# A gated linear recurrence and an MLP on one core: products of token pairs by seven half products, one buffer for the gates, the first pair in two halves

## The chip, the cores and the metric

The kernel runs on one core of a Trainium2 chip. A core has engines that run side by side, each with its own queue in order: TensorE (PE; its weight loads are listed apart as PEld), VectorE (DVE), ScalarE (ACT), GpSimd (POOL), and SyncE (SP), whose queue issues the DMA transfers here. Matrix products go from the on-chip memory SBUF into the accumulators of PSUM, which VectorE and ScalarE read. The metric is the device time of one launch in microseconds, the median of the runs. Before the change it is 813.15 us (three runs, 810.71 to 813.49).

## The reference

Two blocks follow each other. The first is a recurrence for each of 4 batches and 8 heads, over 768 tokens with vectors of 48; its state is a complex 48 x 48 matrix:

```
mag = np.sqrt(a_re * a_re + a_im * a_im)
scale = np.minimum(mag, 0.999) / (mag + 1e-06)
a_re_n, a_im_n = (a_re * scale, a_im * scale)
for t in range(S):
    new_re = ar * S_re - ai * S_im
    new_im = ar * S_im + ai * S_re
    S_re, S_im = (new_re + k[t] (outer) v[t], new_im)
    y[:, :, t] = np.einsum('bhd,bhde->bhe', q[:, :, t], S_re)
```

Its output, as 3072 tokens of 384 numbers, is the input x of the second, an MLP with 2048 features and an own slope for negative values of each feature:

```
h = x @ w_in                                        # 3072 x 384 by 384 x 2048
g = np.maximum(h, 0.0) + alpha * np.minimum(h, 0.0)
return (g @ w_out).astype(np.float32)               # by 2048 x 384
```

All of it is in 32-bit floating point; the large weights arrive as 64-bit words and are turned to 32 bits in the kernel.

## The kernel before

The tokens are cut into 24 units of 128 (six for each batch). Work is written as tasks, Python generators that emit one step at each call:

- `gates` (line 229), nine tasks: for one, two or three units at a time they load the decays `a_re` and `a_im` into the tile `gate`, compute phases and magnitudes with some twenty steps on VectorE and as many on ScalarE, and store phases (`phs`, line 313) and decays with their running products (`decs`, line 350) in DRAM. Most tasks cover three units, half of a batch. The tile has two buffers, so that task g waits only for task g - 2.
- `loads` and `loads_v`: for each unit q and k (tile KQ), the phases (PP), the decays (T) and the rows of v (V and VL).
- `pieces` and `weights`: sixteen pieces of w_in and w_out are loaded into three staging regions (line 410) and turned to 32 bits by ScalarE and VectorE. The regions lie in `g_sb`, the tile that holds the features later.
- `unit` (line 560), one for each unit: VectorE rotates q and k (lines 576, 578) and multiplies decays on at six levels (line 634), TensorE meets keys and queries at each level (line 593, tile ps_lv), masks are put on, keys are transposed (line 705) and multiplied with v (line 717, ps_kv); VectorE brings the state forward (lines 746, 749). The output y of a unit gathers in the PSUM tile ps_y. In the kernel before, four products of zeros open that tile (line 728), then come the 96 products of the masks with v (line 737), and last the products of the states with q (line 761), in two halves: the second needs the state after 64 tokens, so VectorE's line 749. ScalarE copies y out, and it goes to DRAM.
- `loads_x` brings y back as x, with features in the partitions.
- `all_mlp` runs over groups of one or two units (one, one, ten pairs, one, one). `features` (line 809) makes 16 blocks of 128 features for a group: three products into ps_h, then ScalarE (line 816) and VectorE (line 818) make g in `g_sb`. `outputs` (line 828) multiplies a block of one unit with 128 rows of w_out, all 384 columns wide, and sums 16 of them in ps_o; ScalarE copies the sum out (line 838).

The order of all steps is fixed by the string `ORDER`: each letter calls the next step of one task (A to I the gates, J to L the loads, M to O the weights, P to Z and a to m the units, n the x loads, o the MLP). An engine runs its own steps in that order, and waits for what it needs with semaphores. The `R` table names buffers of the planner that made the string; on the chip, the number of buffers of a tile sets what can be reused when.

Of the kernel before, what the change touches and what calls it, by code (L numbers as in the profile page):

```python
# [9 lines left out]
F32 = mybir.dt.float32  # L10
# [3 lines left out]
BF16 = mybir.dt.bfloat16  # L14
# [5 lines left out]
P = 128  # L20
# [11 lines left out]
    "ABAMBMAAAABBAAAAABAAAAAAABMAAAMNNAANBBBBBAAAKKJJJMAAAMJANAAJAAAAAAAABBOBAAONNOOBBBBBOBBBBNNOMOONBPPP"  # L32
    "LJOCKJLLCPCCCNONONPCPPPBBLLLKMMMLLKKBBJBOCPCPNNPBCCPBCBBBBBPPPPNCNBNPNNCPJJLLLLLJLLMJPCBNNPPPNBNBBBP"
    "OPPPPOCOOCPCPPOPPPPPPPMCCNOOOCOOPPDJJJMJJJDCCNNNQDPDODNPPPPDPPQNQCOPQQQQNQCPPMJJMQCOQOQNODOQQDQOJCLL"
    "LMLLLLLQDQNOOCNOORORRRnCLLLLLLLMQDRQRQRQQQQQCRRQQQQDJJKJJJMKoQoQQQoQQQLLLLLLLDONCNRNCCRNOQQOOCQCCQCC"
    "RQRCROCRQNoooooQoDQRQQDoCLooLQooQCLLLLLLRODDDRRRRRoDOoRooooooNRRRRoooRRoNDDDRoooRoRRoRoRRNRSoRSNoDRO"
    "oMJJSoooNooooooRRNSoNNoRRJJRRSSSNooooooooooSSSooooSoSSooODSSoooooSSoOoNooooJJSSnooSoSOSSLJLLLLoooRRL"
    "LLoSDSSTToJLJLLLLLLJEJToSSoSooSOSoTSToOoooTDDDDoOTooooooSSSSSSTTSSSoSToooJJKLLJLLLLoooooTSSSSSTooTTD"
    "ooooToELJJLLooooDoToooooooTDDooooooooTDTTooJLLLJoToooToooUooooooLLUoooDTTTTTooooooooooooooooooooToDD"
    "ooTooDEToooooELTJJJnTooEoTTTDTTToTDDTTTDDooooVUTTEoooooTTTLLFJoEUooUUUVUVLLLooJJoJLLLLJoooUooUoooooo"  # L40
    "ooUooooooUUUooooUUUoooooVoVoUUoooUUoVUUUEooUVEUVoUooUooUoooUoVVEEoEVKJLLLLLUUUUUUUFLLLLLJKKUUUUEVUUU"
    "UVooooooEEooooVVooVoVEEooooVoEoKVoooooooooLLLLLLLLLLVVoEVVoVEoWVoonJJEVVVVooVEEVWVooooooVVVVVVVWoEEo"
    "JLLLLEJLLLEEooooEoWVVVWVWoWEWVEVooVVLLVVoooooWWooooJooEWFooooooooooWWFFLEWEJJJKJLLLJJLLooooooWWWXooo"
    "ooWWWWoXoooooWWWWWFWooWEEFEXEEEoFoooooWWoXooWWWWWWXXoJELLLJLooXWXXXLGLJLoooWWoooXWLLLooXWWXooLXXWWXW"
    "WXoooooooLXXXXXXXXXoooooLLoooooXoXWLGJJoXXooXXXXXoYXoGXYYXooooonJLLJJLKKKLJYoXooYYYYFXXFFYoXXoooYFoo"
    "ooooooYXXFoFoKXJoYYoooGYoYoYFYXFoooooooooFGLLLJLLLLJJJJLLLoooooYYYYYooZoooooZYFFYoooooJLoooYYoFoooYY"
    "ooZGooFFFoooYooZYZZZZoooooooJFFFZYYYYYZFLLLLZLLLFYYYYYYYYYYYoooooooooaYFFFaLLLJoJLJoLLJLLKoooooooKKJ"
    "JJFZZZoooooooZZFZooooooGooZZZZZZZooZZoZooZFFFoaGGooZZooGoaZZZZZoZFZFoFFZFnLLLLLooooooooaZZZZZZZZaGGa"
    "aaZbLFLooooooaooooooaobboooHHJLooaaooooaoooooooabaaooooLJJJLLLLLJoJoooooaaaaaaaaoooaoaooaGGHGaaHoooo"
    "ooooooGbGboGGoooooooaaaaaaaabaaaaaoGboobLLJbboooGbLaaJJHHoooooLLLLLJLLJJLoLoooobcoooooobbGoobbbcbooo"  # L50
    "ooccooooobooHooooobccbbbbbbccooHbbcbooooooooocboobLLLboocGGJnJccbobbbLGGGocbbbdcccdbooooobboLLLLLLLL"
    "LLGGGGGbbbbbobLLLLooccGcoooooocJJJcoHooooococccoGococooooccooooooHoccccccGGGGGcccccccoLLJJJJKLddoGoo"
    "HoGLLLoddoddHdccoccdoooooooooooodeooddodoHdHHdoooooodeoooJJLLLLLLLJJLLJJoooooooodddHHdeoooddoHdoHHed"
    "ddoooeeeedoooIIooddooododdddHddHnddHdddoddooHeeooooddJoooooooIeeeeeoHHeooooooofoeLLdLooooeoeeeoeeeee"
    "ooooJJHJLLLLLoLLLLLLLJJJeoeoofooffoeooJoffofofffooeooooofHHHooeoeIeeeeeeHeeeeeeIgIeIoooooooffooooffo"
    "oooogHffHooHoooooofffoffffHoooeLeLLLLJJLLLLLLLLLLJJJnfJgffooooooooooofoooHgffoggffooofgIJoIHHHHHHogg"
    "gooooofffgffffggffofofgoIggfgoooooIoooooooogghhIIoooooooIogfLLLfhhoooooooIoKLLLJJhJJJJJLLLLLLLLooooh"
    "ooooIIoggoooogohhhhoghggoogoooogoioooggoogggggohggggIIIIooooooggIoggoIooooigLLLgLLLLJJLJhhhJLKoooooo"
    "ooLhhhJJoIJohooooooooooooooohhoooLLLLLihoooohihhhhoohooooiiohhooIIInIohooooooohhhhhhLiihhhhhhhhhhhoo"
    "ooooooiooIIIiioohJJLLLLLLLJJLLLLLLJoooooooIooiiooooooooooiooooiiooooooIiooooooiiIIiiiioiiIooooooojjj"  # L60
    "iooooooIooiooooooijoooijjJJjkooiLikIiooooiiiijjjjoooooiIIiiooooijLLLLLIijiiLoojjjioiLiLijLooooLoLLoo"
    "oojjjoojjjoooojjjooojjooooooojooJLjLLJoojjjjjjjjjJJJJjjjjookjjjjkooooooLookkkkkkooookooooooookkkoook"
    "noooLLLLLJJJLLJLLJJLLLLooooooLllooookkooooooooookkkkkkoooolooookkoookookooookkkoooooookkkkkkkkolllll"
    "lloooooooooooooooooollkkkLlklllJLLLLLLLLLLLoLJoooooooLooookkkkknooooolllooololoooooooooooolllllllJLJ"
    "oooooolooooollloooooooooooooooooollllooooooooolooooooooooooooooooooooooooommmoooooomommmLLLLoooooooo"
    "mmmoooLooooooooooooooooooomolllllllloooommooLlLLlmoooooooooooomnLLLLLmmoooooooooooooooooommmoooooooo"
    "oooommmmmmmooooooooomoooooooooooooooLoooooooooooooooooooooomoooooomooooomoommmmoommmmmmmoooooommmnoo"
    "oooooooooooooooooooooooooooooooooooooooooooooooooooooooooooooooooooooooooooooooooooooooooooooooooooo"
    "ooooooooooooooooooooooooooooooo")
# [28 lines left out]
def kernel(  # L98
# [99 lines left out]
    def step(*args, **kwargs):  # L198
# [5 lines left out]
        KQ=3, PP=1, T=2, V=1, WQ=2, W=1, St=3, xT=2, raw0=1, raw1=1, raw2=1, g0=0, g1=0, g2=0, ot=2, top=2,  # L204
        lv=2, misc=1, y=1, h=2, o=1).items()}
# [3 lines left out]

    scr_of = {}  # L210
# [17 lines left out]

    def gates(g, b, c0, c1):
# [7 lines left out]
        flat = work.tile([P, 6 * NK * GT + 2 * NK], F32, tag="gate", name="gate", bufs=2)  # L237
# [9 lines left out]
        for z, src in ((rows3(x), a_re), (y, a_im)):  # L247
            rows = src[b].rearrange("n i d s -> (n i d) s").rearrange("(t p) s -> p t s", p=P)
            t = yield DMA(N / 2, ("gates", g - 2))
            if last:  # L250
                nc.gpsimd.memset(z[:, :, n - 1:n], 0.0)
            nc.sync.dma_start(z[:, :, 0:n - last], rows[:, :, c0 * P + 1:c1 * P + 1 - last])
            if z is y:
                ty = t
            else:
                tx = t
# [112 lines left out]
    g_sb = consts.tile([P, 3, 6 * MT], F32, tag="g_sb")  # L369

    def region(i):
        return (i + 2) % 3

    def raw_done(name, f, e):

        i = 2 * f + (name == "out")
        for _ in range(6 if i >= NF - 3 else 1):
            R[("g" if i >= NF - 3 else "raw") + str(region(i))].put(e)
# [4 lines left out]
    def pieces():  # L383
# [17 lines left out]
        for f in range(NF // 2):  # L401
            for name, src in (("in", wi), ("out", wo)):
                t = yield DMA(788 if words else 394, takes=(R[f"raw{region(2 * f + (name == 'out'))}"],))
                raw = g_sb[:, region(2 * f + (name == "out"))]
# [148 lines left out]
    nothing = consts.tile([P, D // 2], F32, tag="nothing")  # L553
    nc.gpsimd.memset(nothing, 0.0)
    nothing = nothing.bitcast(BF16)

    sizes = [1, 1] + [MC] * ((NU - 4) // MC) + [1, 1]
    group_of = [(g, c) for g, n in enumerate(sizes) for c in range(n)]

    def unit(u):  # L560
# [159 lines left out]
        for s in range(2):  # L720
            for part in range(2):
                ev = yield PE(0.335 if s or part else 0.44, ("V", u), *(made if not (s or part) else ()), takes=() if s or part else (R["y"],), mode=2, n=12 if s or part else 14)
                if not (s or part):
                    Y = ps.tile([P, 2, 512], F32, tag="y", name="ps_y")[:, :, 0:2 * P].rearrange(
                        "p i (s t) -> p i s t", s=2)
                    for e_ in range(2):
                        for i in range(2):
                            nc.tensor.matmul(Y[64 * e_:64 * e_ + D, i].rearrange("p s t -> p (s t)"),
                                             lhsT=nothing[64 * i:64 * i + 64], rhs=ident.bitcast(BF16)[64 * i:64 * i + 64],
                                             start=True, stop=False)  # L730
                Vp = L["Vp"]
                for h in LEVELS[3 * part:3 * part + 3]:
                    for e_ in range(2):
                        for i in range(2):
                            o = halves(Y[64 * e_:64 * e_ + D, i, s], h)[:, :, 1]
                            a = A[h][64 * i:64 * i + 64, 2 * s + e_]
                            nc.tensor.matmul(o, lhsT=Vp[h][64 * i:64 * i + 64, s, e_ * D:(e_ + 1) * D],  # L737
                                             rhs=a, start=False, stop=False)
        for name in ("V", 1, 4, 16, 32):
            R[name].put(ev)  # L740
# [11 lines left out]
        if not last:  # L752
            state[b] = states[2]
        done["state", u] = k_

        g, cg = group_of[u]
        for s in range(2):
            before, known = states[s]
            e = yield PE(0.47, q_, known, mode=1, n=8)
# [161 lines left out]
```

## Time and profile before

| what | value |
|---|---|
| median of three runs | 813.15 us (810.71 to 813.49) |
| the profiled execution | 812.23 us |
| its span | 810.5 us |
| TensorE busy | 697.3 us, 86% |
| VectorE busy | 564.4 us, 70% |
| ScalarE busy | 457.0 us, 56% |
| mean DMA rate | 161 GB/s |
| granted TensorE clock, mean | 0.975 |

Busy times are unions of an engine's instructions within the span. The ends of matmuls are modelled, so the distance between the starts of neighbours says more about their pace than their durations. A 32-bit product is listed as two records. The time of the execution is 1.7 us more than the span.

### The profile page before, as it was taken

The page shows a single profiled execution, that of the slowest core. Times are in us where ns is not written, and L with a number is a line of the kernel's source. Part 1 is how long each engine was busy: PE and PEld are TensorE (multiplying, and loading weights), DVE is VectorE, ACT ScalarE, POOL GpSimd, SP SyncE. Part 2 cuts the span into 40 slices and gives each one's busy share as a digit, 9 for nine tenths or more (in the row PEclk, how much of TensorE's full clock was granted, in tenths as well). Part 3 has the DMA queues.
Part 4 walks back from the last instruction along what each step waited for, and adds up shares of the span by engine and source line. Part 5 has one row for each costly group of instructions (what it writes and reads, how often), then busy time and mean ns, then how long its engine had stood idle before and what let it go on. Part 6 is the DMA issues. An engine that isn't in the chain of part 4 may idle for free.

```text
span 810.5 us, 26318 instructions
## 1 busy us (share of the span) xinstructions
PE 697.3 (86%) x11488; PEld 522.7 (64%) x11488; DVE 564.4 (70%) x799; ACT 457.0 (56%) x897; POOL 11.9 (1%) x49
## 2 busy tenths in 40 slices
PE   0014167899999999999999999999999999999998
PEld 0013155678777667767777777777777777777776
DVE  6889998878898778786787977887466455154122
ACT  8999894775667447746574558454644333222221
POOL 4000000000000000000000000000000000000000
PEclk9998578999999999999999999999999999999999
DMA  8989998687778596677548765784653743301010
GB/s 231 292 271 249 247 235 225 152 231 200 183 203 212 161 241 141 171 196 176 148 116 228 189 164 139 200 175 114 175 121 101 166 99 100 75 12 36 28 31 10
DMA packets 177578, 130.58 MB, mean 161 GB/s; under 512 B 66296, under 2 KB 168824, under 8 KB 177016
## 3 DMA queue, kind: packets, MB, share of 16 engines
q1 hardware_dynamic: 177464, 128.91, 60.9%
q8 instruction: 90, 1.47, 0.8%
q14 instruction: 24, 0.20, 0.1%
HBM read 100.52 MB, written 35.42 MB: 168 GB/s over the span
## 4 chain that ended last, share of the span: by engine, by line
PE 67%; ACT 14%; DVE 8%; DMA 6%; issue 3%; SPq 2%; POOL 0%; ACTq 0%; DVEq 0%; POOLq 0%
PE ps_o L828 26%; PE ps_h L809 26%; PE ps_lv L593 5%; PE ps_y L737 3%; DVE KQ L634 3%; PE ps_y L761 2%; PE ps_kv L717 2%; DMA T<-decs 2%; PE ps_kt L705 2%; ACT WQ L657 1%; DMA VL<-vsc 1%; DMA PP<-phs 1%; DMA g_sb<-in_w_in_dram 1%; ACT top L426 1%; DVE gate L304 1%
## 5 line engine op out<-in xcount | busy, mean ns | idle before, releaser
L809 PE MATMUL ps_h<-xT,w_in_sb 128*128 128x256 f32 (+1 forms) x1344 | 301.2, 355 | 0.0
L828 PE MATMUL ps_o<-w_out_sb,g_sb 128*128 128x384 f32 x768 | 296.2, 497 | 4.2 <-DVE g_sb L818 3.5
L809 PEld LDWEIGHTS ps_h<-xT,w_in_sb 128*128 128x128 f32 x1344 | 233.1, 192 | 71.3 <-DVE g_sb L818 1.8
L818 DVE SCALAR_TENSOR_TENSOR g_sb<-g_sb,al,ps_h 128x256 f32<-128x256 f32 (+1 forms) x224 | 97.6, 438 | 160.5 <-ACT g_sb L816 160.0
L816 ACT ACTIVATE g_sb<-ps_h 128x256 f32<-128x256 f32 (+1 forms) x224 | 78.4, 352 | 190.9 <-PE ps_h L809 189.9
L634 DVE TENSOR_TENSOR KQ<-KQ,T 96x1024 f32<-96x1024 f32 x120 | 145.9, 1217 | 48.4 <-PE ps_lv L593 38.0
L828 PEld LDWEIGHTS ps_o<-w_out_sb,g_sb 128*128 128x128 f32 x768 | 135.5, 190 | 53.9 <-DVE g_sb L818 6.2
L593 PE MATMUL ps_lv<-WQ 96*32 96x32 f32 x2304 | 34.4, 202 | 56.0 <-DVE WQ L576 38.8
L593 PEld LDWEIGHTS ps_lv<-WQ 96*32 96x32 f32 x2304 | 26.3, 115 | 78.1 <-DVE WQ L576 32.9
L657 ACT COPY WQ<-KQ 96x1024 f32<-96x1024 f32 x48 | 49.9, 1040 | 25.5 <-DVE KQ L634 25.5
L775 ACT COPY T<-ps_y 48x256 f32<-48x256 f32 x96 | 31.6, 364 | 39.7 <-PE ps_y L761 38.9
L737 PE MATMUL ps_y<-A,VL 64*48 64x64 f32 x2304 | 43.8, 225 | 7.3 <-issue 3.7
L607 ACT ACTIVATE A<-ps_lv,columns 128x64 f32<-128x64 f32 x144 | 37.5, 337 | 20.1 <-PE ps_lv L593 20.0
L737 PEld LDWEIGHTS ps_y<-A,VL 64*48 64x48 f32 x2304 | 40.2, 126 | 10.8 <-issue 6.5
L673 ACT COPY W<-KQ 96x512 f32<-96x512 f32 x48 | 30.6, 638 | 28.3 <-DVE KQ L634 27.2
L593 PE MATMUL ps_lv<-KQ,W 96*32 96x32 f32 x1536 | 24.2, 203 | 25.3 <-ACT W L673 24.9
L593 PEld LDWEIGHTS ps_lv<-KQ,W 96*32 96x32 f32 x1536 | 19.4, 114 | 27.8 <-ACT W L673 26.2
L705 PE MATMUL ps_kt<-ident,KQ 96*128 96x96 f32 x192 | 26.0, 260 | 13.0 <-ACT T L708 6.7
L705 PEld LDWEIGHTS ps_kt<-ident,KQ 96*128 96x128 f32 x192 | 20.9, 147 | 23.8 <-ACT T L708 9.1
L707 ACT COPY T<-ps_kt 128x384 f32<-128x384 f32 x48 | 23.1, 480 | 18.8 <-PE ps_kt L705 18.6
L717 PEld LDWEIGHTS ps_kv<-V,T 64*64 64x64 f32 x1408 | 26.6, 142 | 9.5 <-ACT T L708 5.0
L617 DVE TENSOR_TENSOR A<-ps_lv,mask 128x512 f32<-128x512 f32 x48 | 32.7, 681 | 0.0
(85 smaller groups left out, 696.5 us busy)
## 6 DMA issues: line engine op xcount, KB each, us to landing
T<-decs SPq DMA_DIRECT2D x48, 384.0 KB
PP<-phs SPq DMA_DIRECT2D x24, 387.0 KB
KQ<-in_q_dram SPq DMA_DIRECT2D x48, 192.0 KB
phs<-gate SPq DMA_DIRECT2D x14, 577.5 KB
decs<-gate SPq DMA_DIRECT2D x7, 1152.0 KB
KQ<-in_k_dram SPq DMA_DIRECT2D x40, 192.0 KB
vsc<-in_v_dram SPq DMA_DIRECT2D x24, 288.0 KB
VL<-vsc SPq DMA_DIRECT2D x48, 144.0 KB
```

The costliest lines, as they stand in the source:

```text
L593: nc.tensor.matmul(t[64 * i + j:64 * i + j + HC // 2, p], lhsT=keys(n, g), rhs=queries(n, g), start=True, stop=True)
L607: nc.scalar.activation(a[:, :, cols], t[:, :, at:at + name], AF.Copy, scale=s)
L617: nc.vector.tensor_tensor(out=a.rearrange("p l n (g t) -> p l n g t", g=2), in0=t.unsqueeze(3).to_broadcast(whole), in1=pairs[first].rearr ...
L634: nc.vector.tensor_tensor(out=x, in0=x if x0 is None else x0, in1=m, op=ALU.mult)
L657: nc.scalar.copy(z.rearrange("p i n t -> p i (n t)").rearrange("p i (m h) -> p m i h", h=h), bass.AP(tensor=KQ.tensor, offset=KQ.offset + ...
L705: nc.tensor.transpose(t[:, p], KQ[:, 1, 4 * i + p], ident[:D2, :D2])
L717: nc.tensor.matmul(kv[s][j:j + HC, n], lhsT=T[rows, n, j:j + HC], rhs=V[rows, n // 2, (n % 2) * D:(n % 2 + 1) * D], start=True, stop=True)
L737: nc.tensor.matmul(o, lhsT=Vp[h][64 * i:64 * i + 64, s, e_ * D:(e_ + 1) * D], rhs=a, start=False, stop=False)
L809: nc.tensor.matmul(p, lhsT=w_in_sb[:, f // 2, kk, f % 2 * P:(f % 2 + 1) * P], rhs=x_of[m][:, kk], start=(kk == 0), stop=(kk == NK - 1))
L816: nc.scalar.activation(gt, p, AF.Relu, scale=-1.0)
L818: nc.vector.scalar_tensor_tensor(out=gt, in0=gt, scalar=al_1[:, f:f + 1], in1=p, op0=ALU.mult, op1=ALU.add)
L828: nc.tensor.matmul(sums[0], lhsT=gt[:, c * P:(c + 1) * P], rhs=w_out_sb[:, f], start=(f == 0), stop=(f == NF - 1))
```

## The change

Five things are changed together, and the order string is new.

1. For the pairs of units from the third on, the output product is made by a scheme of seven products for a 2 x 2 block product. The two units of the pair are the two block rows of the left matrix, the lower and upper eight feature blocks its columns; w_out is cut into lower and upper features and left and right 192 output columns. Four sums of g blocks (1024 columns each, VectorE) and four differences of weight blocks (made once) feed seven products of 8 x 192 columns; VectorE adds the results up in seven folds, ScalarE copies the first. Both halves of ps_o take turns.
2. The groups are now twelve pairs. The first pair goes through the first eight feature blocks a unit at a time, with its output sums for these kept in `partial`; then the other eight follow for both units, and VectorE adds the two parts.
3. Staging of the weights has four regions, in a shared tile that also holds g, the sums and the differences, and no longer lies over g.
4. The gates have one buffer; the first two tasks share it. Task g waits for task g - 1.
5. The products of zeros are gone: the state products open ps_y, and the 96 products with v follow them.

The core of the diff:

```
-"ABAMBMAAAABBAAAAAABAAAAAAABMAAAMNNAANBBBBBAAAKKJJJMAAAMJANAAJAAAAAAAABBOBAAONNOOBBBBBOBBBBNNOMOONBPPP"
+"ABMABAABAABAAAAABAAAMMMMJAAAAABBAABJNAABJJMBNNAABAKAAKLLLLAAMLMANNAAANAAAAAAANNNNANNBBBBBBBLBBBOOOBB"
...
-        flat = work.tile([P, 6 * NK * GT + 2 * NK], F32, tag="gate", name="gate", bufs=2)
+        if g == 1:
+            flat = room[0][:, 6 * N // C + 2 * NK:]
+        else:
+            flat = room[0] = work.tile([P, GATE], F32, tag="gate", name="gate", bufs=1)
...
-            t = yield DMA(N / 2, ("gates", g - 2))
+            t = yield DMA(N / 2, *[("gates", i) for i in ((0, 1) if g == 2 else (g - 1,)) if g > 1])
...
-    g_sb = consts.tile([P, 3, 6 * MT], F32, tag="g_sb")
-    def region(i):
-        return (i + 2) % 3
+    shared = consts.tile([P, 7 * F2 * P + 3 * F2 * HALF], F32, tag="shared")
+    def region(name, f):
+        i = (2 * f + (name == "out")) % 4
+        at = 18 * MT + i * 4 * DM
+        return R[f"raw{i}"], shared[:, at:at + 4 * DM]
...
-                    for e_ in range(2):
-                        for i in range(2):
-                            nc.tensor.matmul(Y[64 * e_:64 * e_ + D, i].rearrange("p s t -> p (s t)"),
-                                             lhsT=nothing[64 * i:64 * i + 64], rhs=ident.bitcast(BF16)[64 * i:64 * i + 64],
-                                             start=True, stop=False)
...
             for n in range(H):
                 nc.tensor.matmul(Y[64 * (n % 2):64 * (n % 2) + D, n // 4, n // 2 % 2, HC * s:HC * (s + 1)],
                                  lhsT=before[:, n], rhs=KQ[:, 0, n, HC * s:HC * (s + 1)],
-                                 start=False, stop=(s == 1 and n // 2 % 2 == 1))
+                                 start=not s and n // 2 % 2 == 0, stop=False)
...
+    blocks = [(0, f, c, 1) for c in range(MC) for f in range(EARLY)] + [(0, f, 0, MC) for f in range(EARLY, NF)] + [
+        (m, f, 0, MC) for m in range(1, FIRST) for f in range(NF)]
...
+    def twist():
+        for name, dst, x, y, op in (("T3", T3, B22, B12, ALU.subtract), ("T2", T2, T3, B11, ALU.add),
+                                    ("T4", T4, B21, T2, ALU.subtract)):
+            for i in range(2):
+                some = slice(i * F2 // 2, (i + 1) * F2 // 2)
+                nc.vector.tensor_tensor(out=dst[:, some], in0=x[:, some], in1=y[:, some], op=op)
...
+        def product(a, w, name, after):
+            if not bank:
+                bank.append(ps.tile([P, 2, HALF], F32, tag="o", name="ps_o"))
+                bank.append(0)
+            z = bank[0][:, bank[1] % 2]
+            bank[1] += 1
+            for i in range(F2):
+                e = yield PE(0.345, after, known.get(name), takes=() if i else (R["sums"],))
+                nc.tensor.matmul(z, lhsT=a[:, i], rhs=w[:, i], start=i == 0, stop=i == F2 - 1)
+                if i == F2 // 2 - 1:
+                    yield 0
+            return z, e
+        def fold(to, z, e, base, *deps, last=True):
+            t = yield DVE(HALF, e, *deps)
+            STT(out=to, in0=z, scalar=four, in1=base, op0=ALU.mult, op1=ALU.add)
...
+        z, e1 = yield from product(A11, B11, "P1", half)
+        TT(out=apart, in0=A11, in1=A21, op=ALU.subtract)
+        nc.scalar.activation(p1, z, AF.Copy, scale=four)
+        TT(out=A21, in0=A21, in1=A22, op=ALU.add)
+        TT(out=A11, in0=A21, in1=A11, op=ALU.subtract)
+        z, e = yield from product(A12, B21, "P2", full)
+        STT(out=ot[:, 0, 0:HALF], in0=z, scalar=four, in1=p1, op0=ALU.mult, op1=ALU.add)
+        TT(out=A12, in0=A12, in1=A11, op=ALU.subtract)
+        z, e = yield from product(A11, T2, "T2", s2)
+        t2 = yield from fold(u2, z, e, p1, t1)
+        z, e = yield from product(A21, B12, "T1", s2)
+        t3 = yield from fold(v, z, e, u2, t2)
+        z, e = yield from product(apart, T3, "T3", s3)
+        STT(out=ot[:, 1, 0:HALF], in0=z, scalar=four, in1=u2, op0=ALU.mult, op1=ALU.add)
+        tz = yield from fold(ot[:, 1, HALF:DM], z, e, v, t3, ty)
+        z, e = yield from product(A22, T4, "T4", s4)
+        ty = yield from fold(ot[:, 1, 0:HALF], z, e, ot[:, 1, 0:HALF], ty)
+        z, e = yield from product(A12, B22, "P3", s4)
+        t = yield from fold(ot[:, 0, HALF:DM], z, e, v, t3)
```

In the new order a half product (four of the eight) stands between feature blocks of later groups; after the last feature block the remaining six products of the last pair follow each other.

## The prediction

> **What bounds the kernel now.** I read the page first: engine shares, then the span in slices.
>
> ```profile
> span 810.5 us, 26318 instructions
> ...
> PE 697.3 (86%) x11488; PEld 522.7 (64%) x11488; DVE 564.4 (70%) x799; ACT 457.0 (56%) x897; POOL 11.9 (1%) x49
> ...
> PE   0014167899999999999999999999999999999998
> ...
> DVE  6889998878898778786787977887466455154122
> ACT  8999894775667447746574558454644333222221
> ```
>
> TensorE is nearly idle in the first seven slices (some 140 us), while ScalarE and VectorE are at 8 and 9; from then on it is at 9 to the end. So two stages: a start that VectorE, ScalarE and the loads set, and a long stage that TensorE sets. The stretches of 20 us confirm it (PE, PEld, DVE, ACT, POOL, then granted clock, DMA share and GB/s):
>
> ```profile
> 80.00:100.00 20.00, 3.06 (x160) 2.55 (x160) 18.40 (x20) 18.25 (x23) 0.11 (x1) 0.50 0.95 255
> ...
> 220.00:240.00 20.00, 19.58 (x377) 15.04 (x372) 18.48 (x22) 13.40 (x30) 0.11 (x1) 1.00 0.73 182
> ...
> 700.00:720.00 20.00, 20.00 (x145) 14.59 (x144) 6.79 (x12) 3.23 (x9) 0.00 (x0) 1.00 0.11 27
> ```
>
> The clock is 1.00 in the long stage, VectorE is 18.48 of 20 us busy in one stretch without hurting TensorE, and late in the run VectorE has two thirds of its time free. The chain in order of time gives the pace of the large products, with no gap between neighbours:
>
> ```profile
> 470.04 1.29 PE ps_h L809 x6
> 471.34 1.29 PE ps_o L828 x4
> ```
>
> Six records of 256 columns or four of 384 are 1536 columns in 1.29 us: 0.84 ns a column and record, two records a product. The costs of what is added come from the groups by shape (busy us, mean ns, then idle):
>
> ```profile
> L809 PE MATMUL ps_h<-xT,w_in_sb 128*128 128x128 f32 x384 | 58.5, 284 | 0.0
> ...
> L634 DVE TENSOR_TENSOR KQ<-KQ,T 96x1024 f32<-96x1024 f32 x120 | 145.9, 1217 | 48.4 <-PE ps_lv L593 38.0 <-ACT WQ L657 9.2 <-ACT T L775 1.1
> L818 DVE SCALAR_TENSOR_TENSOR g_sb<-g_sb,al,ps_h 128x256 f32<-128x256 f32 x160 | 75.7, 476 | 105.4 <-ACT g_sb L816 105.1
> ...
> L818 DVE SCALAR_TENSOR_TENSOR g_sb<-g_sb,al,ps_h 128x128 f32<-128x128 f32 x64 | 21.9, 344 | 55.2 <-ACT g_sb L816 54.9
> ```
>
> The timeline of the last unit and of the end gives what a handover costs:
>
> ```profile
> 770.12 0.30 PE L728 MATMUL ps_y<-ident,nothing 64*48 64x256 bf16 x4
> 770.25 1.55 PE L737 MATMUL ps_y<-A,VL 64*48 64x64 f32 x96
> 771.46 0.55 DVE L749 TENSOR_TENSOR St<-St,ps_kv 96x384 f32<-96x384 f32 x1
> ...
> 805.06 0.30 PEld L828 LDWEIGHTS ps_o<-w_out_sb,g_sb 128*128 128x128 f32 x2
> 805.17 1.83 PE L828 MATMUL ps_o<-w_out_sb,g_sb 128*128 128x384 f32 x4
> 805.37 0.28 ACT L816 ACTIVATE g_sb<-ps_h 128x128 f32<-128x128 f32 x1 [1.04 <-PE ps_h L809]
> 805.68 0.35 DVE L818 SCALAR_TENSOR_TENSOR g_sb<-g_sb,al,ps_h 128x128 f32<-128x128 f32 x1 [0.97 <-ACT g_sb L816]
> 806.09 0.30 PEld L828 LDWEIGHTS ps_o<-w_out_sb,g_sb 128*128 128x128 f32 x2 [0.72 <-DVE g_sb L818]
> ```
>
> The stream of a finished product ends at 805.17, its reader starts 0.20 us later; TensorE loads 0.06 us after VectorE ends, and multiplies 0.11 us after that.
>
> **The change, part by part** (span 810.5 us, run 812.23 us, so 1.7 us lie around the span; the median of the runs shown is 813.15, 0.9 us above the profiled run).
>
> *Seven products for pairs.* Features are as many columns as before. The output product was 768 records of 384 columns; it becomes 128 of 384 (two pairs kept as they were) and 1120 of 192: 294,912 columns become 264,192. 30,720 x 0.84 ns = **-25.8 us**, on TensorE's path. If instead each narrow record went at the mean of a weight load, about 0.19 us, where 192 columns need 0.161, 1120 x 0.03 = 33 us would be added, +8 in all. I take -25.8: in the tail six records of 128 columns take about 0.66 us, 0.11 each, so loads do not set the pace even there.
>
> VectorE gains, per pair, four sums of 1024 (1.22 us, the row of L634) and seven folds of 192 out of PSUM (0.41, between 0.344 and 0.476): 7.75 us, 77 in ten pairs. Eight operations of 768 on the weights at 0.95 (the gate row of that width) are 7.6; the first pair's two additions 1.2; fewer narrow evictions -4.5. Together +82 on 564, while ScalarE loses 24 copies of 0.49 and gains 14. Beside TensorE this is free as long as VectorE keeps up. In the written order, VectorE's work between the starts of units 8 and 18, summed from row means, rises from 222 to 269 us (sums of means exceed busy time by 7%, so 251 busy), against 269 us of TensorE work between the ends of the same units. At the best stretch's 92% that needs 272 us; at 89%, the mean over 20 to 160 us, 282. **+4**, ends 0 and +13; nearer the first because a good stretch is already shown in the long stage.
>
> The two halves of a product's output tile share one PSUM bank, and in the compiled order each product's first matmul waits for the fold of the product just before it, not of the one before that. A handover costs 0.20 + 0.41 + 0.06 + 0.11 = 0.78 us. Of 69 boundaries, 64 have at least a feature block (1.29 us) between; five, all in the last pair, have nothing: 5 x 0.78 = 3.9. 23 have just one block, and there a sum of 1.22 us ahead in VectorE's queue uncovers at most 0.71: 0 to 16 us. **+6**, ends +4 and +20, near the low end since most folds do not meet a sum. The Trainium skill, PSUM — Partial Sum Buffer, section "PSUM bank collisions raise a hardware error", says that two engines must not touch one bank in the same partitions at once, so that a reader of a bank must be fenced from a writer. By that rule the two halves give no double buffering; if they did, this term would be 0. The compiled waits go by the rule; no run here shows the collision itself.
>
> *State products open y.* 96 opening products go: L737 starts 0.13 us after L728, x 24 units = **-3.1 us** (ends 0 and their 8.2 us of busy time). But the 96 V products (1.5 us) stood between the kv products and the second half of the state products, and covered VectorE's L749. Now they follow. In the order TensorE had at least 2.4 us of work in that gap in every unit; now 0.6 to 3.9, in twelve units at most 1.3. The wait needs about 0.20 + 0.55 + 0.17 = 0.9 us with VectorE free (shortfall 1.5 us in all), and 2.46 as it happened in the last unit, where the queue came late (shortfall 21). **+4**: nearer the low end, since those 2.46 us include VectorE standing idle. Queued behind the state products are the V products, then ScalarE's copy of y, its store and the x load; VL and the A tiles are held some 1.5 us longer.
>
> *First two chunks in halves, weights and gates elsewhere.* Staging no longer shares space with g, has four regions for three, and the first feature blocks need half of the weights. In the order the loads put before unit 4's decays fall from 32.6 to 28.2 MB; at the 249 GB/s of that stage, 18 us. ScalarE's table loads fall from 29 to 20 (1.28 us each). But VectorE, 89% busy there, has as much ahead of units 7 and 8 as before (176 and 215 us become 178 and 217), while TensorE by then has done 4 to 8 us more. **-5**, ends -18 and +3.
>
> The gates get one buffer: the load of a gate's input waits for the store of the one before to land. That wait is on SP; behind it stand V loads and the same gate's decay loads, which need that store anyway. I cost it at 0, covered by the three units (about 82 us) between one gate and the next; uncovered it is the third rival.
>
> Sum: -25.8 - 3.1 + 4 + 6 + 4 - 5 = -19.9: span 790.6, run 792.3; with the median's 0.9, **793 us**.
>
> **Rivals.**
> 1. *The early start is kept*: -18 in place of -5, **780 us**. For it, the loads and table loads; against it, VectorE's unchanged work ahead of unit 8.
> 2. *VectorE is late for everyone*: folds at +20 and its own excess at +13, **816 us**. For it, 251 us busy beside 269 of TensorE; against it, the stretch at 18.48 of 20 with TensorE at 19.58.
> 3. *Slower: one gate buffer.* Full gates' decay stores leave at 125, 193, 266, 360, 441, 520 and 617 us, 82 apart; but load to store took 98 us at best, because two gates overlapped. Alone, a gate is about 20 us on VectorE and 21 on ScalarE, plus loading and landing, so it can fit 82. Each us over 82 counts six times; from 3.3 us over (20 / 6) the gain is gone; at 8 over, +48: **841 us**. The kernel would wait at the first unit of each batch half, in DVE L634's successor.
> 4. *Narrow products at the weight-load pace*: +33, **826 us**; the tail speaks against it.
>
> **How the numbers follow.** Forecast 0.58 (own range 783 to 803), rival 1 0.13, rival 2 0.13, rival 3 0.12, rival 4 0.04. About 0.5% (809 to 817) is what a measurement of this kernel can tell from no change. Faster: 0.58 + 0.13 + 0.05 of rival 2 = 0.76; same: the 0.06 of rival 2 near its price; slower: 0.12 + 0.04 + 0.02 = 0.18. The range reaches to rivals 1 and 2 with some room, 774 to 818, and leaves out rivals 3 and 4.
>
> **What would show it.** The 192-column records start 0.16 us apart (right) or 0.19 (rival 4). TensorE stands at 9 in the slices after the start; the last products are spaced by about 0.8 us of wait for VectorE folds. Waits of state products for L749's successor sum to about 4 us. VectorE's busy time is near 646 us. If decays are late at every third unit, rival 3 holds; if the slices of 200 to 550 us show TensorE at 8 with VectorE at 9, rival 2. The forecast is wrong if the start is as long as before and the folds wait mid-run.

## The result and the profile after

The changed kernel takes **842.21 us** (median of four runs, 837.69 to 844.12) where the kernel before takes 813.32 (810.71 to 814.85). The ratio is 1.035, with an interval of 1.030 to 1.040: slower by 29 us. The forecast was 793, its range ended at 818. The profiled execution of the changed kernel took 837.69 us.

The page of the changed kernel, its shares and its slices:

```profile
span 836.0 us, 26845 instructions
...
PE 699.1 (84%) x11728; PEld 588.2 (70%) x11728; DVE 634.4 (76%) x895; ACT 435.6 (52%) x854; POOL 12.5 (2%) x48
...
PE   0033677899999998988799979988997999999996
...
DVE  6789899897898897877899768676797875762432
```

Before, TensorE stood at 9 from the ninth slice to the last but one. Now it falls to 7 or 8 in eight slices of that stage, and VectorE beside it is mostly at 7 to 9, with 70 us more to do in the whole run than before. The stretch from 190 to 770 us says how much of it is lost (PE, PEld, DVE, ACT, POOL, then granted clock, DMA share and GB/s; of the kernel before the first four were 571.34, 423.25, 396.01 and 294.63, at clock 1.00):

```profile
190.00:770.00 580.00, 539.59 (x9189) 457.30 (x9186) 447.00 (x611) 280.75 (x599) 1.31 (x14) 0.99 0.56 146
```

TensorE stood still for 580 - 540 = 40 us there; before, it was 9. The waits of TensorE in the same stretch (us in total, times, longest us):

```profile
PE ps_o L944 <- DVE top L952: 21.3, 13, 3.6
PE ps_o L944 <- DVE top L973: 11.6, 6, 4.1
PE ps_h L824 <- DVE shared L839: 1.5, 3, 0.6
...
PE ps_y L751 <- DVE St L736: 0.3, 1, 0.3
```

L944 is the product of the seven, L952 and L973 are the folds that read one out of PSUM: 32.9 of the 40 us are products that wait for the fold of the product before them. The wait that the new order of y was to bring (L751 for L736) is 0.3 us. What keeps a fold so long is in the timeline (start, duration, engine, line); here the fold L973 reads product P2, whose last record starts before 480.4, and T2 is the product that waits:

```profile
478.86 1.57 PE L944 MATMUL ps_o<-w_out_sb,shared 128*128 128x192 f32 x8
...
480.35 1.28 PE L751 MATMUL ps_y<-KQ,St 96*48 96x64 f32 x32
...
482.05 1.56 PE L824 MATMUL ps_h<-xT,w_in_sb 128*128 128x256 f32 x6
...
483.90 0.68 DVE L625 TENSOR_TENSOR A<-ps_lv,mask 128x512 f32<-128x512 f32 x1
484.50 0.54 DVE L733 TENSOR_TENSOR St<-St,T 96x384 f32<-96x384 f32 x1
484.96 1.22 DVE L642 TENSOR_TENSOR KQ<-KQ,T 96x1024 f32<-96x1024 f32 x1
486.10 0.54 DVE L736 TENSOR_TENSOR St<-St,ps_kv 96x384 f32<-96x384 f32 x1
...
486.56 1.35 DVE L289 SCALAR_TENSOR_TENSOR gate<-gate 128x1152 f32<-128x1152 f32 x1
...
487.83 0.35 DVE L973 SCALAR_TENSOR_TENSOR top<-ps_o,top 128x192 f32<-128x192 f32 x1
...
488.23 2.93 PE L944 MATMUL ps_o<-shared 128*128 128x192 f32 x8 [4.12 <-DVE top L973]
```

VectorE is busy without a gap and takes the fold in its turn, over 7 us after the product has ended: a mask, a level, two steps of the state and a step of the gates, 4.33 us together, stand straight ahead of it. TensorE has some 3.7 us of other work between the two products (from 480.4 to 484.1: a feature block and steps of a unit), and then its next matmul waits 4.12 us. The eight records after it then run at half pace: they start at 488.23 and the next group starts at 490.95, 2.72 us for what takes 1.30 later in the run.

The same product and the large one, undisturbed:

```profile
788.83 1.46 PE L824 MATMUL ps_h<-xT,w_in_sb 128*128 128x256 f32 x6
...
790.13 1.46 PE L944 MATMUL ps_o<-shared 128*128 128x192 f32 x8
...
791.43 1.46 PE L824 MATMUL ps_h<-xT,w_in_sb 128*128 128x256 f32 x6
```

Eight records of 192 columns in 1.30 us are 0.1625 us each, 0.85 ns a column: the pace that the forecast took.

### The profile page after: what moved, and what is told of

It is laid out like the page before. It is cut to its first block, busy times and chain, and to the rows that moved or that the text cites. A ratio compares the mean times of both kernels' runs of the same rounds, so it can differ in the third digit from the quotient of the medians.

```text
span 836.0 us, 26845 instructions
## 1 busy us (share of the span) xinstructions
PE 699.1 (84%) x11728; PEld 588.2 (70%) x11728; DVE 634.4 (76%) x895; ACT 435.6 (52%) x854; POOL 12.5 (2%) x48
## 5 line engine op out<-in xcount | busy, mean ns | idle before, releaser
L824 PE MATMUL ps_h<-xT,w_in_sb 128*128 128x256 f32 (+1 forms) x1200 | 296.5, 381 | 6.2 <-issue 2.6
L824 PEld LDWEIGHTS ps_h<-xT,w_in_sb 128*128 128x128 f32 x1200 | 218.5, 193 | 40.2 <-issue 5.9
L837 ACT ACTIVATE shared<-ps_h 128x256 f32<-128x256 f32 (+1 forms) x200 | 74.8, 375 | 189.0 <-PE ps_h L824 188.4
L839 DVE SCALAR_TENSOR_TENSOR shared<-shared,al,ps_h 128x256 f32<-128x256 f32 (+1 forms) x200 | 92.4, 464 | 91.6 <-ACT shared L837 91.2
L944 PE MATMUL ps_o<-w_out_sb,shared 128*128 128x192 f32 x640 | 123.5, 332 | 8.6 <-DVE top L952 8.6
L944 PE MATMUL ps_o<-shared 128*128 128x192 f32 x480 | 100.1, 347 | 27.6 <-DVE top L952 14.7
L944 PEld LDWEIGHTS ps_o<-w_out_sb,shared 128*128 128x128 f32 x640 | 105.6, 190 | 15.6 <-DVE top L952 11.3
L944 PEld LDWEIGHTS ps_o<-shared 128*128 128x128 f32 x480 | 82.2, 198 | 36.4 <-DVE top L952 18.5
L854 PE MATMUL ps_o<-w_out_sb,shared 128*128 128x384 f32 x128 | 53.5, 526 | 6.6 <-DVE shared L839 5.6
L854 PEld LDWEIGHTS ps_o<-w_out_sb,shared 128*128 128x128 f32 x128 | 22.9, 197 | 16.2 <-DVE shared L839 8.2
```

The source lines that it names most:

```text
L824: nc.tensor.matmul(p, lhsT=w_in_sb[:, f // 2, kk, f % 2 * P:(f % 2 + 1) * P], rhs=x_of[m][:, kk, c * P:(c + n) * P], start=(kk == 0), stop ...
L837: nc.scalar.activation(gt, p, AF.Relu, scale=-1.0)
L839: nc.vector.scalar_tensor_tensor(out=gt, in0=gt, scalar=al_1[:, f:f + 1], in1=p, op0=ALU.mult, op1=ALU.add)
L854: nc.tensor.matmul(sums[0], lhsT=gt, rhs=w_out_sb[:, f], start=(f == start), stop=(f == stop))
L944: nc.tensor.matmul(z, lhsT=a[:, i], rhs=w[:, i], start=i == 0, stop=i == F2 - 1)
```

## The experiments

Theories at the outset. A: each product waits for the fold of its neighbour, and the folds are late in VectorE's queue. B: VectorE as a whole has too much work. C: another changed wait is to blame, above all the one gate buffer (so the expectations below), or the new order of y. All times below are medians; each ratio is against runs of the kernel before beside it.

| run | what differs from the changed kernel | us | ratio, interval |
|---|---|---|---|
| e1 | folds do not read the product | 792.55 | 0.974 (0.961 to 0.988) |
| e2 | ScalarE takes the product out of PSUM | 815.33 | 1.005 (1.001 to 1.009) |
| e3 | the four sums left out | 836.12 | 1.028 (1.010 to 1.045) |
| e4 | direct products in the places of the seven | 852.55 | 1.048 (1.034 to 1.062) |
| e5 | keys in the bank of y, products in two banks | 802.55 | 0.980 (0.975 to 0.986) |
| e6 | keys in the bank of y, products in one bank | 843.62 | 1.034 (1.029 to 1.039) |
| e7 | the kernel before, with the new order of y alone | 850.18 | 1.043 (1.038 to 1.049) |
| e8 | whole products between blocks, one bank | 832.44 | 1.023 (1.014 to 1.033) |
| e9 | as e5, the old order of y | 846.71 | 1.042 (1.035 to 1.049) |
| e10 | as e5, whole products between blocks | 816.04 | 1.003 (1.000 to 1.006) |

**e1, the wait taken away, the work kept.** The folds read their base where they read the product, at the same width.

```diff
-            STT(out=to, in0=z, scalar=four, in1=base, op0=ALU.mult, op1=ALU.add)
+            STT(out=to, in0=base, scalar=four, in1=base, op0=ALU.mult, op1=ALU.add)
...
-        STT(out=ot[:, 0, 0:HALF], in0=z, scalar=four, in1=p1, op0=ALU.mult, op1=ALU.add)
+        STT(out=ot[:, 0, 0:HALF], in0=p1, scalar=four, in1=p1, op0=ALU.mult, op1=ALU.add)
...
-        STT(out=ot[:, 1, 0:HALF], in0=z, scalar=four, in1=u2, op0=ALU.mult, op1=ALU.add)
+        STT(out=ot[:, 1, 0:HALF], in0=u2, scalar=four, in1=u2, op0=ALU.mult, op1=ALU.add)
```

> The changed kernel, in which the seven folds of a pair read their own base in SBUF a second time in place of the product in PSUM (the products' results are left out of the output). VectorE has the same instructions; only the first product of a pair is still read, by ScalarE. Theory A (a product waits for the fold of the product before it, because both halves of the output tile lie in one PSUM bank, and the fold stands in VectorE's queue behind unit and gate work): the 37 us that TensorE waited for folds go, with some of what follows from them (cold clock, late units): 780 to 805 us. Rival B (VectorE has too much work, the folds are only where it shows): the same work makes TensorE wait elsewhere, 820 us or more. Rival C (one gate buffer sets the pace): 835 to 845 us.

Measured 792.55 us. From its page:

```profile
span 792.1 us, 26829 instructions
...
PE 686.2 (87%) x11728; PEld 583.0 (74%) x11728; DVE 631.6 (80%) x895; ACT 434.4 (55%) x854; POOL 12.5 (2%) x48
...
PE   0033566899999999999999999999999999999999
```

VectorE has the same instructions and nearly the same busy time (631.6 for 634.4), and TensorE is at 9 from the ninth slice to the end. e1 keeps the one gate buffer and the new order of y as well, so neither VectorE's amount of work (B) nor these (C) cost the 50 us. What e1 takes away is the tie between products and folds, and that in both directions: VectorE does not wait for the product either. e5 below, where VectorE still reads every product, prices TensorE's wait alone. Between the two profiled spans, 836.0 and 792.1, lie 43.9 us: TensorE's idle time is 31.0 us less (span less busy: 136.9 and 105.9), and the same matmuls are busy 12.9 us less. Some of the latter is the clock: in four stretches of 20 us of the changed kernel it was 0.91, 0.83, 0.91 and 0.91, in all 8.8 us of clock lost, where in e1 it was 1.00 over 190 to 770 us.

**e2, another engine empties the bank.** ScalarE copies the product out, VectorE folds from the copy.

```diff
-            STT(out=to, in0=z, scalar=four, in1=base, op0=ALU.mult, op1=ALU.add)
+            s = tops[1][:, 3 * HALF:4 * HALF] if base is None else to
+            nc.scalar.copy(s, z)
+            STT(out=to, in0=s, scalar=four, in1=to if base is None else base, op0=ALU.mult, op1=ALU.add)
```

> The changed kernel, with a ScalarE copy of 192 columns that takes each product out of PSUM, and VectorE's fold reading that copy from SBUF: the bank is free when ScalarE has copied, whatever VectorE has ahead. The output is the reference's. Theory A: TensorE's wait for folds turns into a shorter one for ScalarE, 800 to 825 us. Rival B: 830 us or more. Rival C: 835 to 845 us.

Measured 815.33 us. Seventy short copies more on ScalarE, which is 56% busy, take 27 us off. What is left in the stretch of 190 to 770 us:

```profile
PE ps_o L944 <- ACT top L953: 8.2, 5, 2.7
```

The same products wait less when the reader is an engine with less in its queue: 8.7 us with the one other such row (0.5) in place of 32.9.

**e3, less work for VectorE.** The four sums of each pair (1.22 us each) are left out.

```diff
-        TT(out=apart, in0=A11, in1=A21, op=ALU.subtract)
...
-        TT(out=A21, in0=A21, in1=A22, op=ALU.add)
...
-        TT(out=A11, in0=A21, in1=A11, op=ALU.subtract)
...
-        TT(out=A12, in0=A12, in1=A11, op=ALU.subtract)
...
-        z, e = yield from product(apart, T3, "T3", s3)
+        z, e = yield from product(A12, T3, "T3", s3)
```

> The changed kernel without the four sums of 1024 columns for each pair (the products multiply blocks that were not summed, so the output is not the reference's): 49 us less on VectorE, the folds still read PSUM. Theory A: the folds still stand behind unit and gate work; a part of the wait goes, 815 to 832 us. Rival B: the loss goes with the work, 785 to 805 us. Rival C: 835 to 845 us.

Measured 836.12 us, more than theory A expected and inside C's range. It is 6 us less than the changed kernel, but the two executions (832.30 and 839.95) overlap the changed kernel's four, so the gain is not clear of noise. VectorE's busy time falls by 44 us to 590.4, yet in 190 to 770 us the folds are still waited for:

```profile
PE ps_o L944 <- DVE top L952: 20.1, 13, 3.6
PE ps_o L944 <- DVE top L970: 9.0, 4, 3.1
```

So the sums are not the main thing that stands ahead of the late folds; the units' and gates' steps are. In the trace of the changed kernel no sum starts between the start of any of the 19 waits and the fold that ends it. B falls again, and with it the reason that the forecast had for late folds.

**e4, no seven products.** The pairs' outputs go back to 16 products of 384 columns for each row block, put in the places of the seven products' steps; sums and folds go.

```diff
-        z, e1 = yield from product(A11, B11, "P1", half)
+        yield from product(2)
...
+                    nc.tensor.matmul(sums[0], lhsT=spread[:, held[m, f // F2], f % F2, c], rhs=w_out_sb[:, f],
+                                     start=(f == 0), stop=(f == NF - 1))
```

> The changed kernel with the output products of all pairs made directly, 32 products of 384 columns, in the places where the order has the steps of the seven; no sums, folds or weight differences. TensorE has 25.8 us more of work, VectorE 85 us less. The halves of the first pair, the one gate buffer, the staging and the state products first stay. Theory A: the waits for folds go and the added work comes back, 805 to 825 us. Rival B: the same. Rival C: 850 us or more. It tells what the rest of the change is worth: below 813 us it is a gain.

Measured 852.55 us, 28 us above A's and B's range and where rival C put it (850 or more). It is no proof of C: e1 keeps C's causes and takes 792.55 us, and the state products of y wait for VectorE's state for 1.7 us here. Nor does it settle what the rest of the change is worth: 32 products lie in 56 steps, 20 of them crowded into the middle 24, and there are new waits in 190 to 770 us. That the crowding is what makes them was not tested:

```profile
PE ps_h L824 <- DVE shared L839: 7.9, 7, 5.2
PE ps_y L765 <- issue: 6.8, 3, 4.0
PE ps_o L970 <- ACT top L973: 5.9, 8, 2.2
```

**e5 and e6, two banks for the products, and the control.** The keys' transposes move into the bank of y, while no y is open in it; so a second bank is free at times, and successive products take turns between it and the first. One kv product of each unit may take either bank too. e6 makes the same move of the keys, but leaves the products in one bank, each in the same 192 columns.

```diff
+    KT, KV, PR = ['y', 'misc', 'o'], ['misc', 'o'], ['o', 'misc']
...
-            t = ps.tile([P, HP, D2], F32, tag="misc", name="ps_kt")
+            kt_bank, t = bank_of(*KT)
...
-            if not bank:
-                bank.append(ps.tile([P, 2, HALF], F32, tag="o", name="ps_o"))
-                bank.append(0)
-            z = bank[0][:, bank[1] % 2]
-            bank[1] += 1
...
+                if i == 0:
+                    bank[0], z = bank_of(*PR)
+                    z = z[:, 0:HALF]
```

In e6 the three lists read:

```diff
-    KT, KV, PR = ['y', 'misc', 'o'], ['misc', 'o'], ['o', 'misc']
+    KT, KV, PR = ['y', 'misc'], ['misc'], ['o']
```

> The changed kernel with two PSUM banks for the products: the transposed keys go into a bank of ps_y while no y is open, so that the bank they had can take every second product (and one kv product of each unit). Every instruction and its place in the order stay; the output is the reference's. Theory A (a product waits for the fold of the product just before it, since both share a bank): with a bank each, a product waits for the fold before that, which is long done; 792 to 803 us, as without reading PSUM (792.5 us). Rival B (VectorE is too full for the folds, wherever they read): 815 us or more. Rival D (the three users of the two banks now wait for each other): 805 to 825 us, with waits of kt or kv products for folds.

> The same move of the transposed keys into a bank of ps_y, but all products stay in one bank. Theory A: no gain, 832 to 848 us, TensorE's waits for folds at some 30 us as in the changed kernel. If the move of the keys itself is what helped, this comes out near the run with two banks.

Measured 802.55 us (794.62 to 803.31) and 843.62. e5 keeps the whole change and is 2% faster than the kernel before (814.85 beside it; the interval is 1.4 to 2.6%). Its timeline shows the same lateness without the wait: P2 ends, T2 starts 3.8 us before VectorE comes to P2's fold, L999 here.

```profile
469.94 1.57 PE L968 MATMUL ps_x<-w_out_sb,shared 128*128 128x192 f32 x8
...
475.13 1.57 PE L968 MATMUL ps_x<-shared 128*128 128x192 f32 x8
...
478.92 0.35 DVE L999 SCALAR_TENSOR_TENSOR top<-ps_x,top 128x192 f32<-128x192 f32 x1
```

In 190 to 770 us TensorE is busy for 564.79 us of e5 (539.59 in the changed kernel), and the waits for any one line come to 3.6 us at most (seven, for ScalarE's copy W). Rival D shows only once: a kv product waits 1.1 us for a fold. Of e6, in the same stretch:

```profile
PE ps_x L968 <- DVE top L976: 22.4, 13, 3.9
PE ps_x L968 <- DVE top L999: 12.4, 6, 4.1
```

The move of the keys is worth nothing by itself; the second bank is worth 41 us (40 against the changed kernel). So of the 50 us of e1 some 40 are TensorE's wait with what follows from it; the last 10 were not taken apart. The Trainium skill, PSUM — Partial Sum Buffer, section "PSUM bank collisions raise a hardware error", has it that PSUM is to be guarded by bank and not by address. The runs agree as far as they go: with two halves of one bank in turn (the changed kernel, 842.21) or one half alone (e6, 843.62) products wait for the fold just before, with two banks (e5) they do not. The waits are those built into the program: both halves are one tile there, and two tiles in one bank were not tried. The collision itself is in no run here.

**e7 and e9, the order of y.** e7 is the kernel before with the state products first and without the products of zeros, and no other edit; e9 is e5 with the order undone.

```diff
             if not s:
+                Y = ps.tile([P, 2, 512], F32, tag="y", name="ps_y")[:, :, 0:2 * P].rearrange(
+                    "p i (s t) -> p i s t", s=2)
...
-                                 start=False, stop=(s == 1 and n // 2 % 2 == 1))
+                                 start=not s and n // 2 % 2 == 0, stop=False)
+        for s in range(2):
+            for part in range(2):
+                e = ev = yield PE(0.335 if s or part else 0.44, ("V", u), *(made if not (s or part) else ()), takes=() if s or part else (R["y"],), mode=2, n=12 if s or part else 14)
...
```

> The kernel before, with this one part of the change: no products of zeros, the state products open y and the 96 products with v follow, in the steps of the old order. Between the kv products and the second half of the state products TensorE then has 0.6 to 9.1 us of work where it had 2.4 or more, in sixteen units at most 1.2. By the sum of the prediction: -3 us for the products of zeros, +4 to +15 for the wait for VectorE's state: 814 to 825 us. If that wait is hidden: 810 us.

> The kernel with two banks, with the order in y undone: products of zeros open it, the 96 products with v come next, the state products last, in the steps of the new order. It prices that part of the change in the order made for it. By the sum of the prediction the part is worth -3 (products of zeros) and +4 (wait for the state), so this comes out within 5 us of the two-bank kernel, 798 to 808 us. If the part saves more, since the masks may come later now, 810 us or more; if its wait costs what it cost in the old order, below 790 us.

Measured 850.18 and 846.71 us: e7 is 35 us slower than the kernel before, and e9 44 slower than e5. Both lie far outside what the sum of the prediction gave (814 to 825 and 798 to 808); e9 is in the branch of 810 or more that its expectation had for the case that the part saves more in the new string. In 190 to 770 us TensorE stands still for 29.7 us of e7, against 8.7 in the kernel before. In e7 the state products wait mid-run for the state (`ps_y L743` for `St L728`, 7.4 us), and since the V products come later, v's rows are held longer and the loads of the next ones stand on SP. SP's own waits in e7, over the whole run (L539 waited 2.8 us for V products before; how much of the 35 us comes from this is not shown):

```profile
SPq L539 <- PE ps_lv L593: 49.0, 6, 12.1
...
SPq L539 <- PE ps_y L756: 37.3, 6, 29.1
```

In e9 the waits of 190 to 770 us are:

```profile
PE ps_y L794 <- DVE St L780: 19.5, 10, 4.5
PE ps_y L768 <- issue: 8.3, 6, 2.2
```

Either order of the steps of y costs 35 to 44 us in an `ORDER` string that was written for the other. The part has no price of its own that could be carried from one string to the other.

**e8 and e10, more cover in one bank.** A whole product stands after every second feature block, in place of a half product after each. In the order, the smallest work between two products becomes 2.5 us, the mean 3.8 (2.3 before). e8 has one bank, e10 two.

```diff
-                later.append(dict(m=m, steps=seven(m, made), over=False, needs=0))
+                later.append(dict(m=m, steps=seven(m, made), over=False, needs=F2 - 1))
             yield from features(m, f, c, n)
             lag[0] = (m, f, c)
-            yield from some(4 if m == FIRST else 2)
+            yield from some(4 if m == FIRST else 2, 2 * (f % 2))
```

> The changed kernel with one bank as it is, but a whole product (eight matmuls) after every second feature block in place of a half after each: between the end of one product and the start of the next TensorE now has at least 2.5 us of work, 3.8 on average, where it had 1.28 in 23 places and 2.3 on average; only the last five boundaries stay uncovered. The PSUM tile, the instructions and the wait of each product for the fold before it stay. Theory A: the fold has twice the time to come, so of the 33 us of waits in mid-run ten or less stay: 800 to 822 us. Rival B (VectorE too full): 835 us or more, as the work is the same.

> Both: two banks, and whole products after every second feature block. Theory A: no wait for folds is left by the two banks, and nothing is gained by more cover: 795 to 806 us, as with two banks alone.

Measured 832.44 and 816.04 us; both were expected lower. In e8 the fold waits of 190 to 770 us fall from 33 to 10:

```profile
PE ps_o L943 <- DVE top L972: 5.3, 3, 3.5
...
PE ps_o L943 <- DVE top L951: 4.4, 4, 1.7
```

Yet the time falls by 10 only. e10 gives the reason as far as it goes: the regrouping costs 13.5 us where no product waits for a fold (816.04 against 802.55), which leaves 10 of the 23. Its own waits in that stretch are scattered over the units' steps; why the regrouping costs so much was not followed further:

```profile
PE ps_lv L615 <- ACT W L695: 6.1, 8, 1.6
PE ps_h L847 <- DVE shared L862: 4.8, 6, 1.8
PE ps_x L728 <- ACT T L731: 4.7, 4, 1.5
```

## Why the prediction was wrong

**The step that failed** is the fold waits, "+6, ends +4 and +20". It saw the mechanism rightly (one bank, and each product waits for the fold of its neighbour), counted the places where only one feature block covers a fold, and then priced lateness by one instruction: "a sum of 1.22 us ahead in VectorE's queue uncovers at most 0.71". VectorE takes its steps in the order of the string and was 86% busy between 390 and 490 us, so what stood ahead of a fold was a run of steps: 4.33 us in five of them at 488 us, a wait of 4.12. Some of these steps had waits of their own: VectorE stood 1.67 us for decays ahead of the fold that ends the wait of 2.69 at 386 us, and 1.45 us for ScalarE's gate step ahead of that of 3.63 at 640. Mid-run the waits come to 32.9 us instead of "0 to 16", and e3 shows that the sums were the wrong culprits.

The step also looked in too few places. Counted in the trace, the 23 boundaries with one feature block alone have ten waits, 14.1 us in all; that this lies within "0 to 16" is luck, since single waits reach 3.11 where 0.71 was the most allowed. The other 18.8 us fall on nine boundaries with more work between, which the step priced at nothing, the three longest (4.12, 3.81 and 3.63) among them. To this the slower clock is added, 8.8 us over the four stretches, which the step did not have at all. With the tail the whole term is 40 us by e5 and at most 842.2 - 792.5 = 50 by e1, where 6 was forecast.

**The tail's part of that term** was nearly right: 3.9 us for five handovers, 4.6 measured. Three of the last products start 3.32 us after the one before, where 16 records take 2.60, so 0.72 each; the handover with two sums ahead of its fold took 1.41, the one with two folds 0.98:

```profile
819.51 2.87 PE L944 MATMUL ps_o<-w_out_sb,shared 128*128 128x192 f32 x16 [0.45 <-DVE top L952]
...
822.83 2.87 PE L944 MATMUL ps_o<-shared 128*128 128x192 f32 x16 [0.45 <-DVE top L952]
```

**Seven products, -25.8.** The pace held: 0.1625 us a record for the 0.161 that was taken. Rival 4, the pace of weight loads, is refuted. The sum without the fold term is 810.5 - 25.9 = 784.6, with 2.6 for what lies around the span and the median 787; e1 measured 792.55. So all other terms together were 5 us too low.

**The start, -5.** That is about where those 5 us are. The last key transposes of unit 4 start at 153 us (158 before), those of unit 8 at 269 us (264 before; 268 in e1). By then TensorE has done some 4 us more, counted by the columns ahead of that point at 0.84 ns. So by this count the time up to unit 8 that is not spent on columns is the same in e1 as before: the head start of unit 4 is used up, and the term is about 0. No run has this part alone. Rival 1 (780) did not come. (The prediction's "nearly idle in the first seven slices" is too strong: the page gives TensorE 4, 1, 6 and 7 tenths in the fourth to the seventh.)

**The state wait, +4.** 0.3 us of matmul wait in mid-run and 2.0 in the whole run, the rest of it before 100 us. Mid-run it is cheaper than the low end of 1.5; e7 and e9 show that this holds of that string alone.

**VectorE, +4.** Its busy time is 634.4 us, forecast 646. In e1 with the same work TensorE stays at 9, so the amount costs no more than a few us.

**One gate buffer, 0.** About right: the gates took 52 to 101 us from load to store, their stores follow each other at 72 to 108 us, and SP waited 3.2 us in one place for a landing. VectorE waited for decays twice, 1.9 us in all (2.8 before); the longer wait, 1.67 us, is the one at 386 us above. Rival 3 gave 841 us and the time is 842, but not by its mechanism: the likeness is chance.

**Rival 2** (816, at 0.13) was right in one half, folds that are late mid-run, though its +20 is half of what was measured; its other half, VectorE's own excess of +13, did not come.

## What to carry to other kernels

Where a matmul must wait for a reader in a busy in-order engine, price the wait by all that stands in that queue ahead of the reader at that moment, not by the reader and one neighbour; here a VectorE that was 76% busy over the whole run was enough for runs of 4 us. Price it at every place where the product waits, also where more than the least work lies between. If a trace cannot show that queue, leave the upper end of the term open or give the accumulator a second bank: here the bank was worth 41 us, and turned +3.5% into -2%. Here a written order of steps went with the edit it was written for, and the price of one part could not be read off by doing that part alone.

## What the runs showed of the hardware

After the pause of 4.12 us the clock was lower: the stretch around it shows 0.83, and eight records took 2.72 us instead of 1.30.

```profile
480.00:500.00 20.00, 15.16 (x234) 12.41 (x233) 12.95 (x18) 7.25 (x14) 0.11 (x1) 0.83 0.16 30
```

The other three stretches of the changed kernel below 1.00, at 0.91 each, hold the products that came after its next longest waits, 3.81, 3.63 and 3.11 us; the product after a wait of 2.69 us lies in a stretch at 1.00. So these four waits were paid beyond their own length. The Trainium skill, TensorE: Matmul & The Clock Gate, section "What's actually happening", puts the drop to half pace at an idle window of about 3.4 us; the 4.12 us here agree with it, and the 3.11 us are shorter. In e5 the clock was 0.83 from 380 to 400 us, where TensorE's longest wait was 0.79 us, so in these traces a long wait is not the only thing that goes with a lower clock; what else does was not followed.
